# Seven products in the order 1, 6, 5, 2, 3, 7, 4, sums that always read one part from PSUM, one score step at a place, and the last head prepared in one piece

## The chip, the cores and the metric

The kernel runs on one core of a Trainium2 chip. Its engines are TensorE (PE, with its weight loads shown as PEld), VectorE (DVE), ScalarE (ACT), GpSimd (POOL) and SyncE (SP), which issues nearly all DMAs. Each engine works through its own queue in order. The metric is the device time of one execution in microseconds (us).

## The reference

A masked attention is followed by a mixture of experts. Batch 2, 8 heads, 768 rows, head dimension 64; the second part sees 1536 rows of 512, 4 experts, inner width 1024.

```python
q_bits = (np.einsum('bhsd,dk->bhsk', q, proj) > 0)        # the same for k
mask = q_bucket[:, :, :, None] == k_bucket[:, :, None, :]  # bucket: the 6 bits as a number
scores = np.where(mask, scale * np.matmul(q, k.transpose(0, 1, 3, 2)), -1000000000.0)
attn = np.exp(scores - np.max(scores, axis=-1, keepdims=True))
attn = attn / (np.sum(attn, axis=-1, keepdims=True) + 1e-09)
x = np.matmul(attn, v)                                     # heads side by side: 1536 x 512
p = domain_probs / (domain_probs.sum(-1, keepdims=True) + 1e-09)
for e in range(4):
    h = np.maximum(x @ w1[e], 0.0)
    out += p[:, e:e + 1] * (h @ w2[e])
```

## The kernel before

**Stages.** The 16 heads (8 of each batch) pass through attention in steps of 128 rows, six a head: a score step on PE (`stage_s`, L441 and L443, into the PSUM tile `sps`), its clamp and row bound on DVE (L448), the exponential on ACT (L464), a turn of the result on DVE (L528) or PE, DMAs through DRAM, and the product with v on PE (L563, 24 matmuls into `pv`), whose result ACT (L590) and DVE (L588) copy out and POOL scales (L601). The mixture runs as 16 units, eight a batch; a unit is half of an expert's inner width. Its first layer multiplies x by a part of w1, its second layer (`product_2`, L783 to L785, six tiles of 12 matmuls into `mps`) multiplies the hidden values by a part of w2, and DVE adds each tile to `acc` (L777). All matmuls take their operands split into a high and a low part: three matmuls for a product.

**The order.** A program that is written out by hand sets it: `attention()` and `moe(b)` are generators. Each `yield` gives a cost, and after each place of the mixture the loop at the end of the kernel lets attention go on until its summed cost has caught up (`da` against `dm`). So attention of batch 1 runs among units 0 to 4 of batch 0, and what is left is drained in unit 5 (`drained`).

**The last head.** `prep_head` makes the operands of the next head: the scaled copy `ah` on ACT (L370), copies `q` (twice) and `k` of it on POOL (L258), the low part `al` on DVE (L373), `ah`'s first half from `al` on POOL (L258), the signs on ACT (L395, which empty the PSUM tile `hps` of the hash matmuls L385), and two small operations on POOL (L400, L258). For heads up to 14 this goes step by step beside the score steps. The last head (15) shares its tiles with head 14 (`ALONE`), so it is prepared between the last score step of one and the first of the other, with `yield`s in between and a gap of 2100 behind it.

**The fast units.** Units 4 to 15 (`unit_fast`) make the first layer with seven products instead of eight, twice a unit (j = 0 and 1, one half of the unit's width each). A product is 6 matmuls of 384 columns (L1064, L1067, L1068). Numbered by their operands: 1 is a11 b11, 2 a12 b21, 3 s4 b22, 4 a22 t4, 5 s1 t1, 6 s2 t2, 7 s3 t3. Before, their order is 1, 5, 6, 2, 3, 7, 4. Products 1 and 2 collect in the PSUM tile `pa`, 5 and 3 in `pd` (in the first batch all of them are called `mps`), 6, 7 and 4 have a tile each. ACT copies product 1 to SBUF (L1097) and product 5 (L1103); DVE makes the sums (L1107, L1114, L1119, L1120, L1127) in the SBUF tiles `mt`. Product 2 is added onto product 1 and product 3 onto product 5 in PSUM, so each must wait until the value before it has been copied out. A finished sum becomes hidden values: the high part `hh` by a Relu on ACT (`hidden_hi`, L1074), the low part `hl` on DVE (`hidden_lo`, L1079). The last sum of half j = 0 (after product 4) is made hidden in half j = 1, right behind its product 1. Beside that, `split_w2_fast` splits two pieces of w2 in each half, on ACT (L1049) and POOL (L1050). PSUM tiles of the kind `one` go round four buffers.

Of the kernel before, what the change touches and what calls it, by code (L numbers as in the profile page):

```python
# [8 lines left out]
F32 = mybir.dt.float32  # L9
F32R = mybir.dt.float32r  # L10
ACTF = mybir.ActivationFunctionType
ALU = mybir.AluOpType
# [35 lines left out]
SPLIT_FIRST = 3  # L48
FAST = 4
ALONE = 14  # L50
ALONE_GAP = 2100
EARLY = 5


# [1 line left out]
def tile_lsh_attention__then__domain_moe(  # L56
# [273 lines left out]
    def prep_head(b, h):  # L330
# [2 lines left out]

        def copies():
            for rows in (slice(0, D), slice(D, P)):
                copy_pool(q1[rows], ah[0:D].bitcast(F32))
            copy_pool(k2[0:D], ah[D:P].bitcast(F32))

        if second:
# [252 lines left out]
    def stage_m(b, h, g):  # L592
# [16 lines left out]
        if (h, g) == (H - 1, NT // G - 1):  # L609
            done_b[b] = True  # L610

    hseq = [(b, h) for b in range(B) for h in range(H)]
    seq = [(b, h, t) for b, h in hseq for t in range(NT)]
    done_b = [False] * B
# [11 lines left out]
    def attention():  # L626
        n = len(seq)
        prep = [iter(())]

        def do(op, i):  # L630
            if op == "N":
                j = i - LAG_N
                if 0 <= j < n:
                    stage_n(*seq[j])
            elif op == "R":
                for b in range(B):
                    for odd in range(2):
                        j = i - LAG_R[b][odd]
                        if 0 <= j < n and (seq[j][0], seq[j][1] % 2) == (b, odd):
                            stage_r(*seq[j])  # L640
            elif op == "T":
                j = i - LAG_T
                if 0 <= j < n and heavy(*seq[j]):
                    stage_t(*seq[j])
                    return 654
            elif op == "X":
                j = i - LAG_X
                if 0 <= j < n and not heavy(*seq[j]):
                    stage_x(*seq[j])
            elif op == "Y":  # L650
                j = i - LAG_Y
                if 0 <= j < n and j % G == G - 1 and not heavy(*seq[j]):
                    b, h, t = seq[j]
                    stage_y(b, h, t // G)
            elif op == "S":
                if i < n:
                    b, h, t = seq[i]
                    if t == 0:
                        x = hseq.index((b, h))
                        prep[0] = prep_head(*hseq[x + 1]) if x + 1 < len(hseq) else iter(())  # L660
                    stage_s(b, h, t)
                    return 652 + 4270 // NT
                return DRAIN
            elif op == "V":
                for bh, lag in ended(i):
                    for part, at in enumerate(v_lags(*bh)):
                        if lag == at:
                            stage_v(*bh, part, len(v_lags(*bh)))
                            if (bh, part) == ((0, H - 1), len(v_lags(*bh)) - 1):
                                ready[0] = True  # L670
                                return 0
            elif op == "U":
                for bh, lag in ended(i):
                    if lag == u_lag(*bh):
                        stage_u(*bh)
            elif op == "M":
                for (b, h), lag in ended(i):
                    for g in range(NT // G):
                        if h % 2 and lag == (u_lag(b, h) if (b, h) == (0, H - 1) else LAG_M[b] + g):
                            stage_m(b, h, g)  # L680
                if done_b[0] and ready[0]:
                    ready[0] = False
                    return 0
            elif op == "E":
                j = i - LAG_E
                if 0 <= j < n:
                    stage_e(*seq[j])
            elif op == "P":
                if i < n:
                    b, h, t = seq[i]  # L690
                    x = hseq.index((b, h))
                    c = next(prep[0], None) if t >= PREP_AT and x < ALONE else None
                    if t == NT - 1 and x + 2 < len(hseq) and in_blocks(*hseq[x + 2]) and x < ALONE:
                        turn_blocks(*hseq[x + 2])
                    if t == QK_AT and x + 2 < len(hseq):
                        load_qk(*hseq[x + 2])
                    if t == 1 and x:
                        load_v(*hseq[x])
                    return c
            return None  # L700

        for i in range(n + LAG_M[1] + 3):
            for op in ORDER:
                c = do(op, i)
                if c is not None:
                    yield c
            x, t = divmod(i, NT)
            if t == NT - 1 and ALONE <= x < len(hseq) - 1:
                for c in prep[0]:
                    yield c  # L710
                if x + 2 < len(hseq):
                    turn_blocks(*hseq[x + 2])
                yield ALONE_GAP

    wts = {}
    queue = [(g, i, c) for g in range(B * NU) for i in range(2) for c in range(0, KD, WC)]
# [339 lines left out]
    def unit_fast(b, u, first_u):  # L1056
# [33 lines left out]
        w = wts.pop((first_u + u, 0))  # L1090
        sp2 = split_w2_fast(first_u + u)
        ma, mb = (pair_tile([P, 2, SB], "mt") for _ in range(2))
        s1, u2, s5, u3 = ma[:, 0], ma[:, 1], mb[:, 0], mb[:, 1]
        for j in range(2):
            pa = acc("pa", 0)
            product(pa, w["a11"], xop["b11"], j, True)
            nc.scalar.activation(s1, pa, ACTF.Copy)  # L1097
            if j:
                hidden(0, 1 + j, u3)
            yield 1120  # L1100
            pd = acc("pd", 0)
            product(pd, w["s1"], xop["t1"], j, True)
            nc.scalar.activation(s5, pd, ACTF.Copy)  # L1103
            yield 1120
            pb = acc("mps", 1)
            product(pb, w["s2"], xop["t2"], j, True)
            nc.vector.tensor_tensor(out=u2, in0=pb, in1=s1, op=ALU.add)  # L1107
            yield 1120
            product(pa, w["a12"], xop["b21"], j, False)
            hidden(0, j, pa)  # L1110
            next(sp2, 0)
            yield 1120
            product(pd, w["s4"], xop["b22"], j, False)
            nc.vector.tensor_tensor(out=s1, in0=pd, in1=u2, op=ALU.add)  # L1114
            hidden_hi(1, j, s1)
            yield 1120
            pc = acc("mps", 1)
            product(pc, w["s3"], xop["t3"], j, True)
            nc.vector.tensor_tensor(out=u3, in0=pc, in1=u2, op=ALU.add)  # L1119
            nc.vector.tensor_tensor(out=s5, in0=u3, in1=s5, op=ALU.add)  # L1120
            hidden_hi(1, 2 + j, s5)
            hidden_lo(1, j, s1)
            hidden_lo(1, 2 + j, s5)
            yield 1120
            pe_ = acc("mps", 1)
            product(pe_, w["a22"], xop["t4"], j, True)
            nc.vector.tensor_tensor(out=u3, in0=u3, in1=pe_, op=ALU.subtract)  # L1127
            yield 1120
        hidden(0, 3, u3)
        for _ in sp2:  # L1130
            pass
# [8 lines left out]
    with tc.manual_schedule():  # L1140
# [28 lines left out]
        for b in range(B):  # L1169
            dm = da = 0.0  # L1170
            for c in moe(b):
                dm += c
                while da < dm * ATT_PACE * n_att / n_moe:
                    x = next(att, None)
                    if x is None:
                        break
                    da += x
            if b == 0:
                for _ in att:
                    pass  # L1180
# [28 lines left out]
```

## Time and profile before

| | us |
|---|---|
| median of 3 runs (719.26 to 720.13) | 719.74 |
| the profiled execution | 719.53 |
| its span in the profile | 717.6 |
| PE busy | 701.0 (98%) |
| DVE busy | 517.1 (72%) |
| ACT busy | 342.7 (48%) |
| POOL busy | 315.8 (44%) |

Busy time is summed over the span. PE's share is so high that only its idle stretches, and stretches at a lower granted clock, can be told from work that has to be done; where PE waits, the profile names the operation that released it. Attention alone fills the first 125 us or so. From there to about 378 us attention of batch 1 and the mixture of batch 0 share the engines, and from 466.5 us on the second batch's eight fast units follow each other.

### The profile page before, as it was taken

Reading aid. Unit: us, or ns where it says so; the run is one execution under the profiler, and the core shown is the slowest. Engines: PE = TensorE matmul, PEld = TensorE weight load, DVE = VectorE, ACT = ScalarE, POOL = GpSimd, SP = SyncE. Lnnn points to the kernel's source line nnn. Section 1 sums busy time; section 2 is a strip of 40 time slices with the busy share of each in tenths; the row PEclk is TensorE's granted clock in tenths of the full one; section 3 lists DMA queues with packets and bytes.
Section 4 is the critical chain, followed back from the end, with each engine's and each line's share of the span. In section 5 each row is a group of like instructions: output and inputs, shape, how many; then the busy total and the mean of one; then the engine's idle time right before and its main releaser. Section 6 shows DMA issues by size and latency. Waiting matters only on the chain.

```text
span 717.6 us, 10186 instructions
## 1 busy us (share of the span) xinstructions
PE 701.0 (98%) x3702; PEld 590.1 (82%) x3702; DVE 517.1 (72%) x816; ACT 342.7 (48%) x669; POOL 315.8 (44%) x290
## 2 busy tenths in 40 slices
PE   8999999999999999979899999999999999999998
PEld 6766765979888888848687889898998989899896
DVE  6898888856584677767766887866868576685863
ACT  6888787543543434524523344343534334343440
POOL 6359577523363344453324645523434233342420
PEclk9999999999999999979999999999999999999999
DMA  5423353769997797817862112242121221112202
GB/s 137 75 50 74 74 119 79 217 172 239 250 254 204 205 238 207 266 59 202 242 168 61 59 60 89 87 140 67 59 65 64 79 88 60 59 58 89 66 23 88
DMA packets 90849, 87.77 MB, mean 122 GB/s; under 512 B 53168, under 2 KB 55728, under 8 KB 90800
## 3 DMA queue, kind: packets, MB, share of 16 engines
q1 hardware_dynamic: 89776, 86.80, 43.7%
q8 instruction: 29, 0.48, 0.3%
q10 hardware_dynamic: 1024, 0.33, 0.2%
q14 instruction: 20, 0.16, 0.1%
HBM read 65.04 MB, written 22.07 MB: 121 GB/s over the span
## 4 chain that ended last, share of the span: by engine, by line
PE 84%; DVE 5%; POOL 5%; issue 3%; ACT 2%; DMA 1%; POOLq 0%; DVEq 0%; ACTq 0%
PE mps L783 11%; PE mps L785 11%; PE mps L784 11%; PE pv L563 8%; PE mps L1064 4%; PE mps L1068 4%; PE mps L1067 4%; PE sps L443 4%; PE ptps L509 4%; PE sps L441 3%; PE mps L831 3%; PE mps L833 3%; PE mps L832 3%; PE pa L1064 2%; PE pd L1064 2%
## 5 line engine op out<-in xcount | busy, mean ns | idle before, releaser
L785 PE MATMUL mps<-w2hi,hl 128*128 128x512 f32 (+1 forms) x388 | 151.5, 390 | 1.8 <-DVE hl L1079 1.8
L783 PE MATMUL mps<-w2hi,hh 128*128 128x512 f32 (+1 forms) x388 | 152.2, 392 | 0.1
L784 PE MATMUL mps<-w2lo,hh 128*128 128x512 f32 (+1 forms) x388 | 151.4, 390 | 0.0
L1050 POOL TENSOR_TENSOR w2lo<-ws,w2hi 128x512 fp32r<-128x512 f32 x48 | 61.3, 1300 | 152.0 <-ACT w2hi L1049 141.3
L448 DVE TENSOR_SCALAR_CACHE_REDUCE p<-sps 128x768 f32<-128x768 f32 x96 | 90.1, 939 | 19.7 <-PE sps L443 18.0
L777 DVE SCALAR_TENSOR_TENSOR acc<-mps,pe,acc 128x512 f32<-128x512 f32 (+1 forms) x85 | 62.8, 739 | 50.8 <-PE mps L785 50.6
L464 ACT ACTIVATE p<-p,nb 128x768 f32<-128x768 f32 x96 | 89.4, 932 | 19.8 <-DVE p L448 19.4
L785 PEld LDWEIGHTS mps<-w2hi,hl 128*128 128x128 f32 x388 | 73.4, 189 | 18.7 <-DVE hl L1079 2.2
L783 PEld LDWEIGHTS mps<-w2hi,hh 128*128 128x128 f32 x388 | 73.4, 189 | 16.3 <-issue 1.2
L784 PEld LDWEIGHTS mps<-w2lo,hh 128*128 128x128 f32 x388 | 73.5, 189 | 14.1
L1008 POOL TENSOR_TENSOR w1lo<-ws,w1hi 128x512 fp32r<-128x512 f32 x36 | 52.1, 1453 | 53.4 <-issue 41.4
L1074 ACT ACTIVATE hh<-mt 128x384 fp32r<-128x384 f32 x72 | 37.8, 525 | 72.7 <-DVE mt L1120 43.8
L563 PE MATMUL pv<-pt,tv 128*64 128x384 f32 x288 | 67.2, 492 | 0.0
L1004 ACT ACTIVATE w1hi<-wc 128x512 fp32r<-128x512 f32 x48 | 30.1, 631 | 66.5 <-DVE wc L1013 66.4
L441 PE MATMUL sps<-ah,q 128*128 128x384 f32 x192 | 54.1, 363 | 2.6 <-POOL ah L258 2.3
L1079 DVE SCALAR_TENSOR_TENSOR hl<-mt,hh 128x384 fp32r<-128x384 f32 x72 | 42.8, 596 | 16.3 <-ACT hh L1074 13.6
L443 PE MATMUL sps<-k,al 76*128 76x384 f32 x192 | 50.3, 342 | 3.7 <-POOL k L258 3.3
L563 PEld LDWEIGHTS pv<-pt,tv 128*64 128x64 f32 x288 | 24.9, 137 | 32.5 <-issue 31.1
L258 POOL TENSOR_SCALAR q<-ah 64x768 fp32r<-64x768 f32 (+1 forms) x33 | 28.1, 853 | 52.6 <-ACT ah L370 38.4
L528 DVE STREAM_TRANSPOSE t<-p 128x768 f32<-128x768 f32 x48 | 46.2, 963 | 5.9 <-ACT p L464 5.9
L1068 PE MATMUL mps<-xo,w1lo 128*128 128x384 f32 x144 | 48.5, 337 | 0.0
L1067 PE MATMUL mps<-xo,w1hi 128*128 128x384 f32 x144 | 48.4, 336 | 0.0
(158 smaller groups left out, 1555.6 us busy)
## 6 DMA issues: line engine op xcount, KB each, us to landing
ws<-in_moe_w_dram SPq DMA_DIRECT2D x64, 512.0 KB, 3.9
scr<-t SPq DMA_DIRECT2D x16, 1152.0 KB, 8.4
pt<-scr SPq DMA_DIRECT2D x64, 288.0 KB, 6.0
tv<-in_v_dram SPq DMA_DIRECT2D x16, 192.0 KB, 3.0
tqk<-in_q_dram SPq DMA_DIRECT2D x30, 96.0 KB, 3.1
out_dram<-acc SPq DMA_DIRECT2D x11, 256.0 KB, 2.0
tqk<-in_k_dram SPq DMA_DIRECT2D x28, 96.0 KB, 3.3
rdb<-row SPq DMA_DIRECT2D x14, 192.0 KB, 5.6
```

Of the source, the lines that this page charges most:

```text
L441: nc.tensor.matmul(ps[:, i, :NH], q1[:, sl], k1[:, i * NH : (i + 1) * NH], start=True, stop=False)
L443: nc.tensor.matmul(ps[:, i, :NH], q2[0:MQE, sl], k2[0:MQE, i * NH : (i + 1) * NH], start=False, stop=True)
L448: nc.vector.tensor_scalar(out=two(pt), in0=ps[:, :, :NH], scalar1=MASKED, scalar2=MASKED, op0=ALU.min, op1=ALU.min, accum_out=nb,)
L464: nc.scalar.activation(pt, pt, ACTF.Exp, bias=nb, scale=-1.0, accum_out=dens[b, h, r][:, o : o + 1])
L563: nc.tensor.matmul(dst, vvs[b, h][:, c], pts[b, h, g][c], start=c == 0, stop=c == NT - 1, tile_position=(0, g * D),)
L777: nc.vector.scalar_tensor_tensor(out=acc, in0=ps, scalar=pcol, in1=acc, op0=ALU.mult, op1=ALU.add)
L783: nc.tensor.matmul(ps, hh[:, ts], w2hi[:, f, cs], start=n == 0, stop=False)
L784: nc.tensor.matmul(ps, hh[:, ts], w2lo[:, f, cs], start=False, stop=False)
L785: nc.tensor.matmul(ps, hl[:, ts], w2hi[:, f, cs], start=False, stop=n == FC - 1)
L1050: nc.gpsimd.tensor_tensor(out=lo[:, c + o], in0=t[:, o], in1=hi[:, c + o].bitcast(F32), op=ALU.subtract)
L1067: nc.tensor.matmul(ps, whi[:, kk, fs], xl[kk], start=False, stop=False, skip_group_check=True)
L1068: nc.tensor.matmul(ps, wlo[:, kk, fs], xh[kk], start=False, stop=kk == KH - 1, skip_group_check=True)
```

## The change

Five things change.

- In a fast unit product 6 comes before product 5. Product 5 is no longer copied to SBUF by ACT: DVE adds it to the sum of 1 and 6 straight from PSUM (`c22`), and the sum of two SBUF tiles (L1120) becomes a second sum that reads product 7 from PSUM. ACT has one copy less in each half, DVE one sum more.
- The low part `hl` of a hidden value follows its high part at once (`hidden` in place of `hidden_hi` now and `hidden_lo` later).
- A half of a unit has two places for attention (`SLOT` 3920 each) instead of seven (1120 each), and attention makes one score step at a place at most (`S_COST`).
- The last head is prepared in one piece at one place; the costs of its steps are summed onto the gap, which goes from 2100 to 3400.
- The last head's two `q` copies go from POOL to ACT.

```diff
-ALONE_GAP = 2100
+SLOT = 3920
+ALONE_GAP = 3400
@@ prep_head, copies
-                copy_pool(q1[rows], ah[0:D].bitcast(F32))
+                if b * H + h > ALONE:
+                    nc.scalar.activation(q1[rows], ah[0:D].bitcast(F32), ACTF.Copy)
+                else:
+                    copy_pool(q1[rows], ah[0:D].bitcast(F32))
@@ attention
-                for c in prep[0]:
-                    yield c
+                gap = sum(prep[0], ALONE_GAP)
                 if x + 2 < len(hseq):
                     turn_blocks(*hseq[x + 2])
-                yield ALONE_GAP
+                yield gap
@@ unit_fast
-        s1, u2, s5, u3 = ma[:, 0], ma[:, 1], mb[:, 0], mb[:, 1]
+        u2, u3, c12, c22 = ma[:, 0], ma[:, 1], mb[:, 0], mb[:, 1]
         for j in range(2):
             pa = acc("pa", 0)
             product(pa, w["a11"], xop["b11"], j, True)
-            nc.scalar.activation(s1, pa, ACTF.Copy)
+            nc.scalar.activation(u2, pa, ACTF.Copy)
             if j:
                 hidden(0, 1 + j, u3)
-            yield 1120
-            pd = acc("pd", 0)
-            product(pd, w["s1"], xop["t1"], j, True)
-            nc.scalar.activation(s5, pd, ACTF.Copy)
-            yield 1120
+            yield SLOT
             pb = acc("mps", 1)
             product(pb, w["s2"], xop["t2"], j, True)
-            nc.vector.tensor_tensor(out=u2, in0=pb, in1=s1, op=ALU.add)
-            yield 1120
+            nc.vector.tensor_tensor(out=u2, in0=pb, in1=u2, op=ALU.add)
+            pd = acc("pd", 0)
+            product(pd, w["s1"], xop["t1"], j, True)
+            nc.vector.tensor_tensor(out=c22, in0=pd, in1=u2, op=ALU.add)
             product(pa, w["a12"], xop["b21"], j, False)
             hidden(0, j, pa)
             next(sp2, 0)
-            yield 1120
             product(pd, w["s4"], xop["b22"], j, False)
-            nc.vector.tensor_tensor(out=s1, in0=pd, in1=u2, op=ALU.add)
-            hidden_hi(1, j, s1)
-            yield 1120
+            nc.vector.tensor_tensor(out=c12, in0=pd, in1=u2, op=ALU.add)
+            hidden(1, j, c12)
+            yield SLOT
             pc = acc("mps", 1)
             product(pc, w["s3"], xop["t3"], j, True)
             nc.vector.tensor_tensor(out=u3, in0=pc, in1=u2, op=ALU.add)
-            nc.vector.tensor_tensor(out=s5, in0=u3, in1=s5, op=ALU.add)
-            hidden_hi(1, 2 + j, s5)
-            hidden_lo(1, j, s1)
-            hidden_lo(1, 2 + j, s5)
-            yield 1120
+            nc.vector.tensor_tensor(out=c22, in0=pc, in1=c22, op=ALU.add)
+            hidden(1, 2 + j, c22)
             pe_ = acc("mps", 1)
             product(pe_, w["a22"], xop["t4"], j, True)
             nc.vector.tensor_tensor(out=u3, in0=u3, in1=pe_, op=ALU.subtract)
-            yield 1120
@@ the loop at the end
                     da += x
+                    if x == S_COST:
+                        break
```

The instructions move only from the last head's preparation on. Three places follow.

On PE one more second-layer tile, four instead of three, now stands between the last head's hash matmuls and its first score step. On POOL, at that preparation (`q`, `k`, `ah` and `al` are the head's operands, `w1lo` and `w2lo` low parts of weights), the queue before is:

```order
L258 TENSOR_SCALAR q_3338<-ah 64x768 x2
L258 TENSOR_SCALAR k_3341<-ah 64x768
L258 TENSOR_SCALAR ah<-al 64x768
L1008 TENSOR_TENSOR w1lo_3295<-ws,w1hi_3294 128x512
L400 TENSOR_SCALAR al<-k_3341,bit_mul 44x768
L258 TENSOR_SCALAR k_3341<-al 12x768
L1008 TENSOR_TENSOR w1lo_3295<-wc,w1hi_3294 128x512
```

and now:

```order
L259 TENSOR_SCALAR k_3341<-ah 64x768
L259 TENSOR_SCALAR ah<-al 64x768
L404 TENSOR_SCALAR al<-k_3341,bit_mul 44x768
L259 TENSOR_SCALAR k_3341<-al 12x768
L1012 TENSOR_TENSOR w1lo_3295<-ws,w1hi_3294 128x512
```

The two `q` copies are gone to ACT, where they stand between the scaled copy and the signs, and the weight's low part no longer comes between the head's own four operations.

On DVE in unit 4, the one fast unit that shares the engines with score steps (`p<-sps` is the clamp of a score step, `t<-p` a turn, `mt` the sums, `hl` low parts), the queue before is, from the low part of `pa` in half 0 to the first sum of half 1:

```order
L1079 SCALAR_TENSOR_TENSOR hl<-mps,hh 128x384
L1114 TENSOR_TENSOR mt<-mps,mt 128x384
L1119 TENSOR_TENSOR mt<-mps,mt 128x384
L1120 TENSOR_TENSOR mt<-mt 128x384
L1079 SCALAR_TENSOR_TENSOR hl<-mt,hh 128x384 x2
L528 STREAM_TRANSPOSE t_3480<-p 128x6x4x32
L448 TENSOR_SCALAR p,nb<-sps 128x768
L1127 TENSOR_TENSOR mt<-mt,mps 128x384
L1079 SCALAR_TENSOR_TENSOR hl<-mt,hh 128x384
L528 STREAM_TRANSPOSE t_3599<-p 128x6x4x32
L448 TENSOR_SCALAR p,nb<-sps 128x768
L1107 TENSOR_TENSOR mt<-mps,mt 128x384
```

and now, from the sum behind product 7 in half 0 to the sum of product 5 in half 1 (five rows stand ahead of these since product 3: a sum, its low part, the copy of `pv`, a turn and a clamp):

```order
L1120 TENSOR_TENSOR mt<-mps,mt 128x384
L1121 TENSOR_TENSOR mt<-mps,mt 128x384
L1083 SCALAR_TENSOR_TENSOR hl<-mt,hh 128x384
L1125 TENSOR_TENSOR mt<-mt,mps 128x384
L1083 SCALAR_TENSOR_TENSOR hl<-mt,hh 128x384
L479 TENSOR_SCALAR den<-den 128x6
L480 RECIPROCAL rd<-den 128x6
L532 STREAM_TRANSPOSE t_3525<-p 128x6x4x32
L452 TENSOR_SCALAR p,nb<-sps 128x768
L1107 TENSOR_TENSOR mt<-mps,mt 128x384
L1110 TENSOR_TENSOR mt<-mps,mt 128x384
```

The sum that reads product 5 (L1110) is new on DVE and stands behind all of these; before, ACT made the copy that product 3 waits for.

On DVE in a fast unit of the second batch, the queue before is, from the sum behind product 3 of half 0 to the first sum of half 1:

```order
L1114 TENSOR_TENSOR mt<-pd,mt 128x384
L1119 TENSOR_TENSOR mt<-mps,mt 128x384
L1120 TENSOR_TENSOR mt<-mt 128x384
L1079 SCALAR_TENSOR_TENSOR hl<-mt,hh 128x384 x2
L1127 TENSOR_TENSOR mt<-mt,mps 128x384
L1079 SCALAR_TENSOR_TENSOR hl<-mt,hh 128x384
L1107 TENSOR_TENSOR mt<-mps,mt 128x384
```

and now, to the sum of product 5 of half 1:

```order
L1115 TENSOR_TENSOR mt<-pd,mt 128x384
L1083 SCALAR_TENSOR_TENSOR hl<-mt,hh 128x384
L1120 TENSOR_TENSOR mt<-mps,mt 128x384
L1121 TENSOR_TENSOR mt<-mps,mt 128x384
L1083 SCALAR_TENSOR_TENSOR hl<-mt,hh 128x384
L1125 TENSOR_TENSOR mt<-mt,mps 128x384
L1083 SCALAR_TENSOR_TENSOR hl<-mt,hh 128x384
L1107 TENSOR_TENSOR mt<-mps,mt 128x384
L1110 TENSOR_TENSOR mt<-pd,mt 128x384
```

The low part of the first sum has moved ahead of the sum behind product 7, and the row at the end, L1110, is what product 3 of half 1 waits for.

## Rows read from the trace of the kernel before

**Rows 1.** Waits of PE: releaser, us in total, times, longest us.

```profile
PE mps L1064 <- ACT mt L1103: 2.4, 1, 2.4
...
PE mps L785 <- DVE hl L1079: 1.8, 1, 1.8
```

**Rows 2.** Timeline of PE, 307.7 to 321: start, duration, instruction, idle before.

```profile
307.74 0.39 PE L783 MATMUL mps<-w2hi,hh 128*128 128x512 f32 x1
...
308.19 0.39 PE L785 MATMUL mps<-w2hi,hl 128*128 128x512 f32 x1
310.84 1.01 PE L441 MATMUL sps<-ah,q 128*128 128x384 f32 x2 [2.27 <-POOL ah L258]
314.79 1.01 PE L443 MATMUL sps<-k,al 76*128 76x384 f32 x2 [2.94 <-POOL k L258]
315.59 0.63 PE L783 MATMUL mps<-w2hi,hh 128*128 128x512 f32 x1
...
320.85 4.14 PE L563 MATMUL pv<-pt,tv 128*64 128x384 f32 x24
```

**Rows 3.** Windows: length, busy us of PE, PEld, DVE, ACT, POOL, granted clock, DMA.

```profile
310.00:312.00 2.00, 1.01 (x2) 0.50 (x2) 2.00 (x4) 1.24 (x3) 1.92 (x2) 0.69 0.19 57
...
340.00:342.00 2.00, 0.32 (x2) 0.00 (x0) 1.41 (x4) 1.11 (x2) 0.00 (x0) 1.00 1.05 221
...
497.40:528.30 30.90, 30.90 (x157) 28.04 (x157) 21.93 (x31) 12.28 (x23) 11.09 (x8) 1.00 0.22 69
```

**Rows 4.** Timeline of ACT, DVE and POOL at the last head's preparation.

```profile
304.59 0.92 ACT L370 ACTIVATE ah<-xt,qk_scale 128x768 fp32r<-128x768 f32 x1
...
305.54 1.18 ACT L395 ACTIVATE k<-hps,sgn_bias 44x384 fp32r<-44x384 f32 x2
305.60 2.70 POOL L258 TENSOR_SCALAR q<-ah 64x768 fp32r<-64x768 f32 x2 [3.05 <-ACT ah L370]
306.03 1.58 DVE L373 SCALAR_TENSOR_TENSOR al<-xt,qk_scale,ah 128x768 fp32r<-128x768 f32 x1
...
309.53 1.26 POOL L258 TENSOR_SCALAR ah<-al 64x768 fp32r<-64x768 f32 x1
...
312.60 1.22 POOL L400 TENSOR_SCALAR al<-k,bit_mul 44x768 fp32r<-44x768 f32 x1
...
313.90 0.83 POOL L258 TENSOR_SCALAR k<-al 12x768 fp32r<-12x768 f32 x1
```

**Rows 5.** Groups of DVE: count, busy us, mean ns of one, idle before.

```profile
L448 DVE TENSOR_SCALAR_CACHE_REDUCE p<-sps 128x768 f32<-128x768 f32 x96 | 90.1, 939 | 19.7 <-PE sps L443 18.0
...
L528 DVE STREAM_TRANSPOSE t<-p 128x768 f32<-128x768 f32 x48 | 46.2, 963 | 5.9 <-ACT p L464 5.9
...
L1120 DVE TENSOR_TENSOR mt<-mt 128x384 f32<-128x384 f32 x24 | 32.3, 1348 | 0.8
```

**Rows 6.** Timelines of DVE, POOL and ACT in the fast unit that starts at 497.46.

```profile
502.86 0.56 DVE L1114 TENSOR_TENSOR mt<-pd,mt 128x384 f32<-128x384 f32 x1
...
504.49 1.45 DVE L1120 TENSOR_TENSOR mt<-mt 128x384 f32<-128x384 f32 x1
...
502.96 2.56 POOL L1050 TENSOR_TENSOR w2lo<-ws,w2hi 128x512 fp32r<-128x512 f32 x2 [8.22 <-ACT w2hi L1049]
...
515.99 2.99 POOL L1008 TENSOR_TENSOR w1lo<-ws,w1hi 128x512 fp32r<-128x512 f32 x2 [3.24 <-issue]
...
516.50 1.33 DVE L1013 TENSOR_TENSOR wc<-ws 128x512 f32<-128x512 f32 x1
...
503.45 0.53 ACT L1074 ACTIVATE hh<-mt 128x384 fp32r<-128x384 f32 x1
...
508.02 0.47 ACT L1103 ACTIVATE mt<-pd 128x384 f32<-128x384 f32 x1
```

**Rows 7.** Timeline of PE in the same unit: products 2 and 3 of half 1 start.

```profile
507.86 0.34 PE L1064 MATMUL pa<-xo,w1hi 128*128 128x384 f32 x1
...
508.90 0.34 PE L1064 MATMUL pd<-xo,w1hi 128*128 128x384 f32 x1
```

More of the change, by code (lines that the diff above doesn't have):

```diff
@@ L610, in stage_m @@
             done_b[b] = True
+    S_COST = 652 + 4270 // NT
     hseq = [(b, h) for b in range(B) for h in range(H)]
@@ L661, in do @@
                     stage_s(b, h, t)
-                    return 652 + 4270 // NT
+                    return S_COST
                 return DRAIN
@@ L1096, in unit_fast @@
             product(pa, w["a11"], xop["b11"], j, True)
-            nc.scalar.activation(s1, pa, ACTF.Copy)
+            nc.scalar.activation(u2, pa, ACTF.Copy)
             if j:
                 hidden(0, 1 + j, u3)
-            yield 1120
+            yield SLOT
+            pb = acc("mps", 1)
+            product(pb, w["s2"], xop["t2"], j, True)
+            nc.vector.tensor_tensor(out=u2, in0=pb, in1=u2, op=ALU.add)
             pd = acc("pd", 0)
             product(pd, w["s1"], xop["t1"], j, True)
-            nc.scalar.activation(s5, pd, ACTF.Copy)
-            yield 1120
-            pb = acc("mps", 1)
-            product(pb, w["s2"], xop["t2"], j, True)
-            nc.vector.tensor_tensor(out=u2, in0=pb, in1=s1, op=ALU.add)
-            yield 1120
+            nc.vector.tensor_tensor(out=c22, in0=pd, in1=u2, op=ALU.add)
             product(pa, w["a12"], xop["b21"], j, False)
```

## The prediction

> **What bounds the kernel now.** I read the waits of PE first. PE is busy for 98% of the span, so only its few idle stretches can be won, and any new one is paid in full. Two of the larger waits stand in [rows 1]: 2.43 us in unit 4, where product 3 waits for ACT's copy of product 5, and 1.78 in unit 5, where a second-layer matmul waits for a low part `hl`. The other two are in the timeline of PE at the last head's preparation [rows 2]: 2.27 before the first half of the score step, and 2.94 before the second. I read the windows next [rows 3]. Behind those waits the granted clock is 0.69 of full and then 0.5, that is, the lower of its two levels, and a second-layer matmul takes 0.63 where it took 0.39. In unit 4, with 1.68 of 2 us idle, the clock stays at 1.00. The last window is a whole fast unit of the second batch, with PE busy 30.90 of 30.90 us. There are ten such units (6 and 7 of the first batch, eight of the second), and none has anything to win. What the change does to them can only be nothing or a loss. Last I read the timelines of the other engines, since every term below is a race of one of them against PE.
>
> **The last head.** From the end of the tile before (its last start 308.19, plus 0.39) to the product with v (320.85) PE spends 12.27 us. The work in it is one tile, 12 matmuls at 0.227 each (three starts apart 0.45 for two), 2.72, and the score step, four matmuls of 384 columns at 0.173 (a sixth of the pitch of a product, 1.04, [rows 7]), 0.70. So 8.85 is lost: 5.21 idle, 3.64 by the clock.
>
> Now the change [rows 4]. The two `q` copies leave POOL (2.70), and no weight part stands between POOL's four operations. On ACT the `q` copies cost about 0.92 each, as the scaled copy L370 of twice the partitions and equal length does. ACT ends `ah` at 305.51, the copies at 307.35, the signs (1.18) at 308.5. On POOL the first `k` copy and `ah` from `al` are over by 308.9 (`al` ends at 307.6, plus 1.26), the bit product (1.22) by 310.1, the last copy (0.83) by 310.95. PE has one more tile to do meanwhile: 308.42 + 2.72 = 311.14. The cover is thin, 0.2 us, and the fourth tile may wait some 0.1 to 0.3 for the PSUM tile that the signs empty at 308.5. I take **−8.5**, between −8.85 and −5.2 (a short wait that still brings the lower clock, 3.64). If the cover is gone, every tenth of POOL's chain is a tenth of PE's.
>
> **Unit 4.** Here DVE also serves score steps. Before, product 3 of half 1 waits 2.43 for ACT. After, it waits for DVE's new sum L1110, which queues behind everything from product 3 of half 0 on: eight sums and low parts, the copy of `pv`, itself, ten rows at 0.56 [rows 6], 5.6; two turns at 0.96 and two clamps at 0.94 [rows 5], 3.8; and two Relus of ACT at 0.53 that low parts wait for, with hand-offs 1.35 by estimate. That is 10.75. PE has in that time six products at 1.04 and two score steps at 0.70, 7.65, so it waits 3.1. Behind it I add three smaller waits of one DVE row each (a PSUM tile that a late row empties, the next tile, the first second-layer tile), 1.6. So 4.7 in place of 2.4, **+2.3**. The ends: −2.4, if DVE's rows overlap more than I think, and +5.
>
> **Unit 5.** The low part of the first sum now comes at once, ahead of the sums behind product 7. I take 0.5 in place of 1.78, **−1.3** (−1.8 to 0).
>
> **The ten full units.** This is the term that decides. Take the traced unit's times [rows 6]. Half 0's sum c12 runs on DVE from 502.86 to 503.42. ACT's Relu of it ends at 503.98 (it stands behind the two `w2hi` copies, as before). DVE's next row is now its low part, which reads two SBUF tiles while POOL is busy from 502.96 with the first of two subtractions of 1.28 each, until 504.24. The trace shows what such a row does beside POOL: L1120 begins at 504.49 and takes 1.45, to 505.94, that is 0.42 past POOL's end at 505.52. So the low part ends near 504.24 + 0.42 = 504.66. Then follow on DVE, each behind the one before: the sum behind product 7, 505.22; the new `c22`, 505.78; its Relu on ACT, 506.31; its low part, 506.87; the sum behind product 4, 507.43; its Relu, 507.96; its low part, 508.52; product 6's sum of half 1, 509.08; and L1110, 509.64, or some 0.1 less by overlap of neighbouring rows. PE could start product 3 of half 1 at 508.90 [rows 7], as it does now (ACT's copy ended at 508.49, 0.41 before). So PE waits 0.65 to 0.75, once a unit. Half 0 has no such wait: DVE has been idle before it. At the second layer's start a low part of half 1, held up by POOL in the same way, is late by about 0.2. Together 0.9 a unit, **+9.0** for ten. The ends are 0 and 2.1 a unit (0.9 and the 1.28 of POOL's second subtraction, rounded), 0 to +21.
>
> The Trainium skill, "SBUF — State Buffer", section "SBUF: two separate sides", says that VectorE and GpSimd share one pair of ports by an exclusive lock: a VectorE row with two SBUF inputs and a GpSimd row that reads SBUF do not overlap, and the one that starts later waits for the whole of the other. The trace agrees in L1120's mean of 1.35 over 24 [rows 5]. The rule speaks against this change, since it moves a row of that kind into POOL's stretch; if POOL's second subtraction, too, counts as started first, the rule gives rival C's time in place of the sum's.
>
> **The clock.** Three us of idle in unit 4 may bring the lower clock. 2.43 idle did not [rows 1, 3], 2.27 and 2.94 close together did, and cost 3.64. I take **+0.8**, 0 to +3.6.
>
> **Removed and added for nothing.** ACT's 24 copies of 0.47 go and no one waited for them but in unit 4; PE's instructions are the same in number; the places for attention change what runs ahead of what only from the last head on.
>
> **Sum.** −8.5 + 2.3 − 1.3 + 9.0 + 0.8 = +2.3. On the profiled execution (719.53; span 717.6 and 1.9 around it) that is 721.8, and with the median 0.21 above that execution, **722.0**.
>
> **Rivals.**
> - *A, the other side: no wait in the full units.* DVE reaches L1110 by 508.90, with 6.04 us behind c12's start where I count 6.7. It decides at that one point: if the rows that follow each other overlap by 0.1 each, 0.7 goes. Then 722.0 − 9.0 = 713.0. Against it: three Relus stand inside the chain, and their hand-offs are only partly in my count.
> - *B: the low part is not held by POOL.* Then 0.45 a unit, 722.0 − 4.5 = 717.5. Against it is L1120's 1.45; for it, that L1120 is a sum, and these rows show no low part that starts beside a POOL row.
> - *C: POOL's second subtraction goes first as well,* and the low part ends 1.28 later; about 1.1 a unit more, 733.0. Against it: at 515.99 two POOL rows take 2.99 where two take 2.56 otherwise, with a DVE row of 1.33 started at 516.50 [rows 6], so DVE gets in between two of POOL's.
> - *D: the lower clock lasts in unit 4,* +3.6 in place of 0.8: 724.8.
> - That the change does not do what it says is excluded for the order, which the queues show. That the last head gains less is in its bounds.
>
> **How the numbers follow.** The forecast has 0.50, with a range of its own from 718.5 to 726 (0.6 to 1.2 a unit, and unit 4 by its bounds); A 0.17, B 0.15, C 0.06, D 0.12. From 714.0 to 727.5 the range takes in B, D, the forecast and the upper part of A (0.1 of a wait left a unit), and leaves out C and most of A, 0.19. A measurement of this kernel can tell about 0.2% from no change, 718.3 to 721.2. Faster is A, two thirds of B and a little of the forecast, 0.29; the same is the rest of B and the forecast's lower part, 0.20; slower 0.51.
>
> **What would show it.** In the profile after: PE's wait for L1110 at product 3, some ten times 0.65 and one of about 3 in unit 4; no wait of note at the last score step and the clock at 1.00 near 310; unit 5's wait for `hl` at a third; the second sum behind product 7 at 0.56, and the low part of c12 ending 0.4 past a POOL subtraction. I am wrong on the whole if full units show no wait of PE, or if the last head's chain still ends behind the tile.

## The result, and the profile after

The changed kernel takes 723.57 us (median of 4 runs, 723.31 to 723.66) against 719.62 (719.26 to 720.13) for the kernel before on the same chip: a ratio of 1.0054, interval 1.0036 to 1.0071. It is slower by 3.9 us; the forecast was 722.0, slower by 2.3. The profiled execution took 723.31, its span is 721.6 against 717.6. On the chip of the repeat below the executions of the kernel before run from 719.3 us, at a mean granted clock of 0.994, to 722.9, at 0.990, so ratios from two chips can be compared to some 2 us and no closer.

PE's busy time, 705.1 us, is again 98% of the span, so the sum shows nothing. The waits do. From the view of PE's waits after the change (releaser, us in total, times, longest us; L1068 is a matmul of a product, L1110 the new sum):

```profile
PE mps L1068 <- DVE mt L1110: 4.4, 3, 3.7
PE pd L1068 <- DVE mt L1110: 4.0, 8, 0.5
...
PE sps L447 <- POOL k L259: 0.4, 1, 0.4
```

None of the waits of [rows 1] is left. In their place PE waits for the new sum L1110: once in each of the eight units of the second batch, 0.50 as the profile counts it, and three times in the first batch, in units 4, 6 and 7. The last head's waits are down to 0.4.

**The full units.** The same unit as in [rows 3], in the windows view (length, busy us of PE, PEld, DVE, ACT, POOL, granted clock, DMA):

```profile
495.27:527.07 31.80, 31.30 (x157) 27.92 (x156) 21.80 (x33) 11.17 (x21) 11.37 (x8) 1.00 0.21 67
```

A unit is 31.80 long where it was 30.92, with the granted clock at 1.00. DVE is not busier than before (21.80 against 21.93): two sums of two SBUF tiles, 1.45 and 1.39, are gone and four sums of 0.56 have come, and still the unit is longer. The timelines of DVE, POOL and PE between the first sum of half 0 and product 3 of half 1 (start, duration, instruction, idle before):

```profile
500.67 0.56 DVE L1115 TENSOR_TENSOR mt<-pd,mt 128x384 f32<-128x384 f32 x1
501.82 0.67 DVE L1083 SCALAR_TENSOR_TENSOR hl<-mt,hh 128x384 fp32r<-128x384 f32 x1 [0.59 <-ACT hh L1078]
502.41 0.55 DVE L1120 TENSOR_TENSOR mt<-mps,mt 128x384 f32<-128x384 f32 x1
502.88 0.54 DVE L1121 TENSOR_TENSOR mt<-mps,mt 128x384 f32<-128x384 f32 x1
504.01 0.56 DVE L1083 SCALAR_TENSOR_TENSOR hl<-mt,hh 128x384 fp32r<-128x384 f32 x1 [0.59 <-ACT hh L1078]
504.49 0.55 DVE L1125 TENSOR_TENSOR mt<-mt,mps 128x384 f32<-128x384 f32 x1
505.62 0.56 DVE L1083 SCALAR_TENSOR_TENSOR hl<-mt,hh 128x384 fp32r<-128x384 f32 x1 [0.59 <-ACT hh L1078]
506.10 0.55 DVE L1107 TENSOR_TENSOR mt<-mps,mt 128x384 f32<-128x384 f32 x1
506.76 0.56 DVE L1110 TENSOR_TENSOR mt<-pd,mt 128x384 f32<-128x384 f32 x1
...
500.77 2.87 POOL L1054 TENSOR_TENSOR w2lo<-ws,w2hi 128x512 fp32r<-128x512 f32 x2 [8.12 <-ACT w2hi L1053]
...
506.53 0.34 PE L1072 MATMUL pa<-xo,w1lo 128*128 128x384 f32 x1
507.37 0.44 PE L1068 MATMUL pd<-xo,w1hi 128*128 128x384 f32 x1 [0.50 <-DVE mt L1110]
```

From the start of the first sum (500.67) to the end of L1110 (507.32) are 6.65 us. DVE stands still three times in it, 0.59 each, for a Relu of ACT. Between the start of the last matmul of product 2 and that of the first of product 3 are 0.84, where two starts are normally 0.17 apart (the pitch), so the true wait is 0.67; "0.50" is what is left after the modelled end of the matmul before. The matmul that restarts costs 0.11 more, and the first second-layer tile another 0.08: 0.86 of the unit's growth of 0.88.

**The last head.** On PE the fourth tile ends and the score step starts at 312.32; its second half and the next work follow (timeline of PE):

```profile
312.32 0.51 PE L445 MATMUL sps<-ah,q 128*128 128x384 f32 x2
312.86 0.61 PE L447 MATMUL sps<-k,al 76*128 76x384 f32 x2
313.31 0.34 PE L1068 MATMUL mps<-xs,w1hi 128*128 128x384 f32 x1
```

The step takes 0.99 instead of the 0.70 of its matmuls alone, and the window from 300 to 320 has the clock at 1.00 where [rows 3] had 0.69. Of the 8.85 us lost before [rows 2], 0.29 are left.

**Unit 4.** The timelines of DVE and PE ahead of product 3 of half 1, and the windows of PE behind it (length, busy us, granted clock):

```profile
331.49 0.56 DVE L1083 SCALAR_TENSOR_TENSOR hl<-mt,hh 128x384 fp32r<-128x384 f32 x1 [0.59 <-ACT hh L1078]
331.96 0.17 DVE L479 TENSOR_SCALAR den<-den 128x6 f32<-128x6 f32 x1
332.16 0.19 DVE L480 RECIPROCAL rd<-den 128x6 f32<-128x6 f32 x1
332.40 0.98 DVE L532 STREAM_TRANSPOSE t<-p 128x768 f32<-128x768 f32 x1
333.31 0.92 DVE L452 TENSOR_SCALAR_CACHE_REDUCE p<-sps 128x768 f32<-128x768 f32 x1
...
334.16 0.55 DVE L1107 TENSOR_TENSOR mt<-mps,mt 128x384 f32<-128x384 f32 x1
334.81 0.56 DVE L1110 TENSOR_TENSOR mt<-mps,mt 128x384 f32<-128x384 f32 x1
...
335.43 0.69 PE L1068 MATMUL mps<-xs,w1hi 128*128 128x384 f32 x1 [3.72 <-DVE mt L1110]
```

```profile
335.40:337.00 1.60, 1.57 (x5) 0.50 0.22 22
337.00:338.60 1.60, 1.60 (x7) 0.54 0.84 252
338.60:340.00 1.40, 1.40 (x10) 1.00 0.82 195
```

A turn and a clamp of a score step stand right ahead of the two sums, and PE waits 3.9 us (4.06 between the starts less 0.17), then works at the lower clock (0.50 and 0.54 granted) for 3.2 us.

**Where the 4.0 us of span came from.** The starts of the fast units in the two traces give the stages:

| stage | change, us | forecast |
|---|---|---|
| up to 190 us: a product with v waits for a transfer | +1.1 | – |
| last head, up to its first score step | −8.6 | −8.5 |
| from there to unit 5 (366.58 before, 362.77 after) | +3.7 | +2.3 and +0.8 |
| unit 5 | −1.7 | −1.3 |
| units 6 and 7 | +2.5 | +1.8 |
| the eight units of the second batch | +7.0 | +7.2 |

The first line stands at a place where the change moves nothing; whether it belongs to the change is asked below.

### The profile page after: what moved, and what is told of

It reads as the page before. It is cut to its first block, busy times and chain, and to the rows that moved or that the text cites. A ratio compares the mean times of both kernels' runs of the same rounds, so it can differ in the third digit from the quotient of the medians.

```text
span 721.6 us, 10160 instructions
## 1 busy us (share of the span) xinstructions
PE 705.1 (98%) x3702; PEld 588.1 (82%) x3702; DVE 515.4 (71%) x840; ACT 331.8 (46%) x647; POOL 317.9 (44%) x288
## 4 chain that ended last, share of the span: by engine, by line
PE 74%; DVE 14%; ACT 6%; DMA 2%; issue 2%; POOL 1%; SPq 0%; DVEq 0%; POOLq 0%; ACTq 0%
PE mps L787 11%; PE mps L789 10%; PE mps L788 10%; PE pv L567 9%; PE ptps L513 4%; PE sps L447 4%; PE sps L445 4%; DVE hl L1083 4%; ACT hh L1078 4%; PE mps L835 3%; PE mps L1068 3%; PE mps L837 3%; PE mps L836 3%; PE mps L1072 2%; PE mps L1071 2%
## 5 line engine op out<-in xcount | busy, mean ns | idle before, releaser
L1054 POOL TENSOR_TENSOR w2lo<-ws,w2hi 128x512 fp32r<-128x512 f32 x48 | 65.5, 1387 | 141.1 <-ACT w2hi L1053 139.8
L1083 DVE SCALAR_TENSOR_TENSOR hl<-mt,hh 128x384 fp32r<-128x384 f32 x72 | 46.9, 652 | 42.6 <-ACT hh L1078 42.6
L1068 PE MATMUL mps<-xo,w1hi 128*128 128x384 f32 x144 | 48.5, 337 | 0.0
L1071 PE MATMUL mps<-xo,w1hi 128*128 128x384 f32 x144 | 48.4, 336 | 0.0
```

What stands on the lines that cost most here:

```text
L1054: nc.gpsimd.tensor_tensor(out=lo[:, c + o], in0=t[:, o], in1=hi[:, c + o].bitcast(F32), op=ALU.subtract)
L1068: nc.tensor.matmul(ps, whi[:, kk, fs], xh[kk], start=first and kk == 0, stop=False, skip_group_check=True)
L1083: nc.vector.scalar_tensor_tensor(out=hl, in0=src, scalar=0.0, in1=hh.bitcast(F32), op0=ALU.max, op1=ALU.subtract)
```

## The experiments

The kernel before took 719.6 us on the first chip and 721.1 to 721.8 on those of the experiments, so each is given beside the kernel before of its own chip.

**The two parts apart.** First the last head's part alone on the kernel before (diff against the kernel before; the `q` copies on ACT as in the change):

```diff
+ALONE_GAP = 3400
-                for c in prep[0]:
-                    yield c
+                gap = sum(prep[0], ALONE_GAP)
...
-                yield ALONE_GAP
+                yield gap
```

> The kernel before with only the last head's part of the change: prepared in one piece, gap 3400, its two q copies on ACT; the fast units and their places as before. If the last head's 8.85 us are won as a part of their own, and the loss of the whole change sits in the fast units: 719.6 - 8.5 = 711, with a spread of 3 since a sixth score step now falls into unit 4. Rival: what is won there comes back later, because the score steps that PE no longer waits for only crowd unit 4: 717 to 720.

Measured 710.95 us beside 721.37, ratio 0.9862 (0.9843 to 0.9881). Then the rest alone, the change with this part undone:

> The changed kernel with the last head prepared as before (step by step, gap 2100, q copies on POOL). If the two parts add up: 723.6 + 8.5 = 732, full units 0.9 us longer each than before, PE's 2.3 and 2.9 us waits at the last head back. Rival: the parts overlap (the waits of unit 4 shrink when its score steps come later): 728 or less.

Measured 731.96 beside 721.37, ratio 1.0155 (1.0133 to 1.0177). Gain and loss are separate: −10.4 and +10.6 us on that chip. They add up to +0.2, under the whole (+3.9 on the first chip, +1.8 in the repeat below) by no more than chips differ. In the last head's part alone all of PE's remaining waits are small (view of PE's waits):

```profile
PE sps L444 <- DVE p L451: 1.8, 2, 1.5
```

The larger of the two, 1.5, is a score step in unit 4 that waits for the clamp of one before. In the other kernel, with the units alone, the waits for L1108 (there the number of L1110) and the old waits at the last head stand side by side:

```profile
PE mps L1066 <- DVE mt L1108: 7.0, 4, 3.7
PE pd L1066 <- DVE mt L1108: 4.4, 8, 0.9
PE sps L444 <- POOL k L259: 3.7, 2, 3.3
PE sps L442 <- POOL ah L259: 2.3, 1, 2.3
```

**The chain to L1110.** In half 1, the low part of half 0's last sum goes behind L1110 (diff against the changed kernel):

```diff
             if j:
-                hidden(0, 1 + j, u3)
+                hidden_hi(0, 1 + j, u3)
...
             nc.vector.tensor_tensor(out=c22, in0=pd, in1=u2, op=ALU.add)
+            if j:
+                hidden_lo(0, 1 + j, u3)
             product(pa, w["a12"], xop["b21"], j, False)
```

> The changed kernel, but in half 1 the low part of the last sum of half 0 is made behind the new sum L1110, not ahead of it (its Relu stays where it is). Theory, that the chain of ten DVE rows from the first sum to L1110 sets product 3 of half 1 in each full unit: the low part (0.56) and the Relu it waits for (0.53 and a hand-off) leave the chain, L1110 ends some 1.0 us sooner, ahead of PE, so its wait of 0.67 and the restart go: 723.6 - 10 x 0.78 = 715.8, and about 1 less in unit 4: 715. Rival 1, that the DVE is simply full in half 1, so that the row moved delays the rows behind it as much: within 2 of 723.6. Rival 2, that the low part held up by POOL is what is late: no change in the chain's start, so 720 or more.

Measured 714.50 beside 721.37, ratio 0.9912 (0.989 to 0.9935). A full unit of the second batch is as long as before the change, PE full:

```profile
493.50:524.39 30.89, 30.89 (x157) 28.08 (x156) 20.79 (x33) 11.28 (x21) 11.34 (x8) 1.00 0.22 68
```

The chain of nine rows (the expectation counted ten) ended 0.67 late; with one row of 0.56 and the Relu that it waits for out of it, the whole loss of these eight units is gone. DVE has room for the new sums, it only must not have them in this order. In units 6 and 7, which had grown by 1.4 and 1.1, 0.5 and 0.3 are left: there product 2 of half 0 still waits for ACT's copy of product 1. In unit 4 nothing was won, against the expectation: PE's wait is still 3.7. The timelines of DVE and ACT there tell why (in this kernel the turn ahead of the two sums, and what ACT does before it):

```profile
331.27 0.98 DVE L532 STREAM_TRANSPOSE t<-p 128x768 f32<-128x768 f32 x1 [1.20 <-ACT p L468]
...
329.79 0.53 ACT L1078 ACTIVATE hh<-mt 128x384 fp32r<-128x384 f32 x1 [0.71 <-DVE mt L1127]
330.22 0.92 ACT L468 ACTIVATE p<-p,nb 128x768 f32<-128x768 f32 x1
```

The low part is gone from its front, and DVE stands idle for 1.20 in its stead: the turn waits for ACT's exponential, and this stands in ACT's queue behind the Relu of half 0's last sum, which the edit left in its place. The turn starts 1.05 behind the last matmul of product 2, as late as in the changed kernel (1.03).

**The new sum itself.** Product 5 is copied out by ACT again (diff against the changed kernel):

```diff
-            nc.vector.tensor_tensor(out=c22, in0=pd, in1=u2, op=ALU.add)
+            nc.scalar.activation(c22, pd, ACTF.Copy)
...
-            nc.vector.tensor_tensor(out=c22, in0=pc, in1=c22, op=ALU.add)
+            nc.vector.tensor_tensor(out=c22, in0=u3, in1=c22, op=ALU.add)
```

> The changed kernel, but product 5 is copied out by ACT again, and the second sum behind product 7 is again the sum of two SBUF tiles; order of products, low parts and places as changed. Theory: L1110 (0.56) and its place behind product 6's sum leave DVE, but the SBUF sum meets POOL's second subtraction and ends about 0.6 later, so PE's wait in a full unit is 0.1 to 0.3 in place of 0.67: 723.6 - 5 = 718.6. Rival, that the order 1, 6, 5 is what costs: no gain, 723 to 725. Rival, that the added sum is the whole cost: no wait left, 715.

Measured 717.34 beside 721.37, ratio 0.9948 (0.993 to 0.9966). A full unit is 31.19, 0.3 longer than before the change:

```profile
492.29:523.48 31.19, 31.19 (x157) 27.87 (x156) 21.18 (x31) 12.17 (x23) 11.57 (x8) 1.00 0.20 68
```

The order 1, 6, 5 is not what costs, as it is kept here, and putting the copy back on ACT wins back two thirds of the unit's 0.88. What is left is not at product 3, where the expectation had it: 0.06 is lost there, and 0.19 at the second layer's first tile. The SBUF sum met POOL's second subtraction, as expected:

```profile
500.01 1.07 DVE L1121 TENSOR_TENSOR mt<-mt 128x384 f32<-128x384 f32 x1
...
497.80 2.87 POOL L1054 TENSOR_TENSOR w2lo<-ws,w2hi 128x512 fp32r<-128x512 f32 x2 [8.13 <-ACT w2hi L1053]
```

It ends at 501.08, 0.41 past POOL's end at 500.67.

**POOL's stretch.** The split of w2 starts later in each half (diff against the changed kernel):

```diff
             hidden(0, j, pa)
-            next(sp2, 0)
...
             hidden(1, j, c12)
+            next(sp2, 0)
```

> The changed kernel with the first split of w2 in each half moved from behind the Relu and low part of product 2's sum to behind those of product 3's, so that POOL's two subtractions start some 1.2 us later; nothing else. The low part of c12 is then free of POOL (0.11 us won), and the low part of c22, which reads two SBUF tiles too, starts while POOL is in its second subtraction. If such a row waits for the whole of POOL's row, as in unit 6 of one profile, it ends some 0.85 later, and with it all rows to L1110: PE's wait in a full unit goes from 0.67 to about 1.4, and 723.5 + 10 x 0.75 = 731. If VectorE and GpSimd rows only share and both slow a little: within 1.5 of 723.5. If POOL's stretch plays no part: the same as the changed kernel or 1 less.

Measured 742.84 beside 721.10, ratio 1.0293 (1.0264 to 1.0322): in the direction expected, and more of it. The DVE row that now meets POOL's stretch, and POOL's:

```profile
517.39 1.51 DVE L1083 SCALAR_TENSOR_TENSOR hl<-mt,hh 128x384 fp32r<-128x384 f32 x1 [0.59 <-ACT hh L1078]
...
515.93 2.55 POOL L1054 TENSOR_TENSOR w2lo<-ws,w2hi 128x512 fp32r<-128x512 f32 x2 [8.82 <-ACT w2hi L1053]
```

And of PE's waits in this kernel:

```profile
PE pd L1068 <- DVE mt L1110: 10.7, 8, 1.3
...
PE pv L567 <- DMA pt<-scr: 3.0, 1, 3.0
PE mps L1068 <- ACT mt L1101: 1.8, 2, 1.6
```

The low part ends at 518.90, 0.42 past POOL's end, 0.95 late. PE's wait at product 3 is 1.33 in place of 0.50, 0.83 more where 0.75 was expected. The unit is 2.06 longer than before the change, and not 1.65, because the same row of half 1 is held as well, which I had not priced: the first second-layer tile waits for it. The two profiles differ by 21.6 us: 9.3 in the eight units of the second batch, and 12.3 in units 4 to 7, where other work shares the engines. Of these, 3.0 are a product with v that stood for a transfer and 1.6 a wait for ACT's copy; the rest I did not follow up, so this run bears out the expected mechanism in the eight units and not its total.

**Unit 4's score step.** The first of a half's two places for attention goes behind L1110 (diff against the changed kernel):

```diff
-            yield SLOT
             pb = acc("mps", 1)
...
             nc.vector.tensor_tensor(out=c22, in0=pd, in1=u2, op=ALU.add)
+            yield SLOT
             product(pa, w["a12"], xop["b21"], j, False)
```

> The changed kernel with the first of a half's two places for attention moved from behind product 1 to behind the new sum L1110, so that in unit 4 the turn and the clamp of a score step stand behind that sum on DVE, not ahead of it. Nothing else; the full units have no attention in them and do not change. Theory, that unit 4's wait of 3.9 comes from these two rows, which themselves wait for ACT's exponential: the wait falls to about 1.7 (the low part ahead of the sum is still there), the lower clock behind it (1.6) goes, so 723.5 - 3.9 = 719.6. Rival, that the score steps only trade places and PE then waits for a clamp instead: within 1.5 of 723.5.

Measured 721.95 beside 721.78, ratio 1.0009 (0.9998 to 1.0021), and the changed kernel on the same chip:

> The changed kernel once more, on the chip of the next two, as their reference and for one question: in its first profile the product with v at 185.5 us stood still some 0.8 us for a transfer, at a place where the change moves nothing. If that was chance, this profile does not have it, and the span is about 1.1 shorter beside the kernel before (a ratio of 1.004); if it comes from the change, it is there again (1.0055).

723.53 beside 721.78, ratio 1.0026 (1.0014 to 1.0038). So the place is worth 1.6 us and not 3.9, close to what the rival had. PE's timeline in unit 4 with the later place:

```profile
328.65 0.44 PE L1068 MATMUL mps<-xs,w1hi 128*128 128x384 f32 x1 [0.83 <-DVE mt L1121]
...
332.55 0.44 PE L1068 MATMUL mps<-xs,w1hi 128*128 128x384 f32 x1 [0.81 <-DVE mt L1109]
...
340.33 0.51 PE L787 MATMUL mps<-w2hi,hh 128*128 128x512 f32 x1 [1.58 <-ACT hh L1078]
```

The 3.7 at product 3 have become 0.81 (L1109 is L1110 there), but two other waits grew. Product 5 waits 0.83 for L1121, which empties its PSUM tile (0.12 in the first trace): the score step that stood ahead of it on PE now comes after it. The second layer waits 1.58 for a Relu whose sum stands behind the turns and clamps on DVE. The lower clock did not come.

The repeat answers its question. Its product with v at the same place runs through in one piece (timeline of PE),

```profile
185.91 4.09 PE L567 MATMUL pv<-pt,tv 128*64 128x384 f32 x24
```

so the 1.1 us in the first line of the table was chance. From the start of unit 0 to that of unit 2, where all eleven runs have the same instructions, the first trace takes 98.3 us and eight of the others 97.2. The expectation's other half failed: the repeat's span is not 1.1 shorter but 0.9 longer (722.5), and the ratio is below both of its values. In unit 4 the lower clock lasted longer, up to 340.7 us, and cost 2.8 where it had cost 1.5. And unit 6 shows something that the first trace does not (timelines of DVE and POOL in the repeat):

```profile
406.13 1.70 DVE L1083 SCALAR_TENSOR_TENSOR hl<-mt,hh 128x384 fp32r<-128x384 f32 x1 [0.59 <-ACT hh L1078]
...
404.86 2.55 POOL L1054 TENSOR_TENSOR w2lo<-ws,w2hi 128x512 fp32r<-128x512 f32 x2 [1.01 <-ACT w2hi L1053]
```

and in the first trace:

```profile
405.67 0.56 DVE L1083 SCALAR_TENSOR_TENSOR hl<-mt,hh 128x384 fp32r<-128x384 f32 x1 [0.59 <-ACT hh L1078]
...
404.44 2.94 POOL L1054 TENSOR_TENSOR w2lo<-ws,w2hi 128x512 fp32r<-128x512 f32 x2 [1.04 <-ACT w2hi L1053]
```

In the repeat the low part of c12 began when POOL's first subtraction ended, and was held through the second, to 407.83, 0.42 past its end. In the first trace the same row was not held, and POOL's pair took longer. PE's wait behind it was 1.49 in the repeat and 0.34 in the first trace. The kernel with the last head's part undone and the one with the later place show the 1.49 in unit 6 as well.

**Both edits of the units together.**

> Both edits: the low part of half 0's last sum behind L1110, and the first place behind it too. Theory: no wait in the full units, and nothing of note at product 3 in unit 4: 714.5 - 3.9 - 1.6 = 709, a ratio of 0.983 to 0.985 to the kernel before, with the last head's gain kept; that would be below the last head's part alone (0.986). Rival, as for the run before: 713 to 715, a ratio near 0.991.

Measured 714.03 beside 721.78, ratio 0.9887 (0.9868 to 0.9906): between the two, nearer the rival. Its unit 4 has 1.98 of wait at the second layer, with the lower clock behind it, and 0.83 at product 5, in place of 3.7 at product 3. It does not reach the last head's part alone.

**What wins at the last head.** The last head's part alone, with the `q` copies left on POOL (diff against that kernel):

```diff
-                if b * H + h > ALONE:
-                    nc.scalar.activation(q1[rows], ah[0:D].bitcast(F32), ACTF.Copy)
-                else:
-                    copy_pool(q1[rows], ah[0:D].bitcast(F32))
+                copy_pool(q1[rows], ah[0:D].bitcast(F32))
```

> The last head's part alone (one piece, gap 3400, fast units as before), but with its two q copies left on POOL. Theory, that the one piece with its fourth tile covers the chain only because the copies left POOL: POOL's last copy ends 2.7 later, near 315, PE waits some 2.3 at the second half of the score step, with or without the lower clock behind it: 711 + 2.4 = 713.4 to 715.5 (a ratio of 0.989 to 0.992). Rival, that the one piece alone, with the weight's low part out of POOL's chain, is what wins: 711 again (0.986).

Measured 713.85 beside 721.10, ratio 0.99 (0.9876 to 0.9924), 2.7 us more than with the copies on ACT by the ratios. POOL's chain ends late and PE waits for it:

```profile
312.94 1.22 POOL L258 TENSOR_SCALAR k<-al 12x768 fp32r<-12x768 f32 x1
...
314.21 0.62 PE L443 MATMUL sps<-k,al 76*128 76x384 f32 x2 [1.84 <-POOL k L258]
```

So the larger part of the gain, 7.2 us, is the one piece with its tile more and a POOL queue without the weight's part (these two were not tried apart); moving the copies closes what is left.

## Why the prediction was right

**The last head, −8.5:** −8.6, but the size came by another way than the sum's. The two copies on ACT took 1.70 together and not 1.84, and `ah` from `al` 0.83 and not 1.26, but two operations of POOL took longer, its last copy among them (timeline of POOL):

```profile
311.63 1.18 POOL L259 TENSOR_SCALAR k<-al 12x768 fp32r<-12x768 f32 x1
```

The sum had 0.83 for this one, and 1.22 for the bit product ahead of it, which took 1.74. POOL ended at 312.81 and not 310.95, the tile at 312.32 and not 311.14 (1.1 of both the chance wait ahead). So the chain does end behind the tile, by 0.49, which the prediction gives as a sign that it is wrong on the whole: the cover of 0.2 was not there. It cost only 0.3, since the first half of the score step does not need POOL's last copy and runs meanwhile, and since the lower clock did not follow. The margin of 0.35 in −8.5 was taken with a wait of the fourth tile for the signs in mind, which did not come. Here the size was right in part by luck.

**The ten full units, +9.0:** +9.5. In the eight of the second batch the place, the releaser and the size were right: 0.67 of wait forecast as 0.65 to 0.75, and L1110's end 6.65 behind the start of the first sum where the sum had 6.7. Two small terms went against each other in it: the three hand-offs to a Relu took 0.59 where 0.53 stood in the sum, and rows that follow each other overlap by some 0.08. The 0.2 at the second layer was 0.08, and the restarting matmul's 0.11, which is not in the sum, made up for it. That moving one row takes the loss of these units away entirely shows the chain to be the cause. Units 6 and 7 grew by 1.4 and 1.1 and not by 0.9: L1110 costs 0.51 and a restart there, and product 2 of half 0 waits 0.3 to 0.4 for ACT's copy of product 1, which the forecast does not have. Rival A, without a wait in the full units, did not come, but the kernel with the low part behind L1110 met its condition in the second batch, and the price was about the one named: 9.0 forecast, 8 to 10 by the ratios (0.9912 against 1.0026 and 1.0054).

**Rival B was mispriced.** With the forecast's own numbers the low part that is not held ends at 503.98 + 0.56 = 504.54 and a hand-off, against 504.66 when it is held: 0.1 a unit, and not 0.45. The trace has 0.67 for it where 0.56 is free. It could never have brought the time to 717.5, and its 0.15 of chance belonged to the forecast.

**Rival C happened in unit 6.** There POOL's second subtraction went first in the repeat and in two kernels more, and PE's wait was 1.15 longer (1.49 against 0.34), forecast as 1.1; of the four traces with the changed kernel's chain to L1110 only the first was spared. The Trainium skill, "SBUF — State Buffer", section "SBUF: two separate sides", has it that of a VectorE row with two SBUF inputs and a GpSimd row that reads SBUF the one that starts first holds the shared ports for its whole instruction. The traces agree: every row held through a second subtraction here ends 0.41 to 0.42 past it. Who goes first when POOL has its next row waiting, they show too: in the eight units of the second batch DVE did, in both traces (0.67 or 0.68 in each), in unit 6 it was one or the other (the last section has the starts).

**Unit 4, +2.3 and +0.8 for the clock:** +3.7. The wait was 3.9 and not 3.1, since the chain has three gaps of 0.59 and one of 0.36 (for the exponential) where the sum took 1.35 for two; the three smaller waits came to 0.9 and not 1.6. The lower clock cost 1.5: six matmuls of product 3 and the score step of four at up to 0.32 pitch in place of 0.17, and the restart. The wait before, counted by the pitch too, was 2.6 and not 2.4. In the repeat the clock cost 2.8 and the smaller waits 0.4; both clock figures lie between the 0.8 taken and rival D's 3.6. The step that was incomplete is the list itself: it had the rows of DVE, and not ACT's Relu and exponential that the turn among them waits for, which is why taking a row out of the list moved nothing there.

**Unit 5, −1.3:** −1.7; the wait that was left at 0.5 did not come at all. **Chance, not in the sum:** +1.1 by a transfer in the profiled execution. Without it the forecast of +2.3 stands against +2.9 in that trace. Other chances went the other way in it: in the repeat unit 6 is 0.9 longer and unit 4 0.7. That the total lies so near the forecast is in part luck.

**A version that beats both** is the last head's part without the rest, 0.9862 of the kernel before. The sums from PSUM with the low part behind L1110 come to 0.9912: no loss in the eight units any more, but no gain either, as PE had none to give; most of the distance to 0.9862 is unit 4, 49.9 us long against 46.6.

## What to carry to other kernels

When PE has no idle time in a stage, work that is taken off DVE there is worth nothing (a unit was 30.9 long with DVE busy for 21.93 and for 20.79), and an added row is paid if it lands on the one chain that ends at PE's next release: follow that chain row by row, with every hand-off to another engine (0.59 of idle here for a Relu of 0.53), before counting busy time. A result that PE needs soon goes ahead of the one that is needed late; here the order of two rows on DVE was worth 8 to 10 us, a whole new sum less than that (5.6 to 7.6 by the ratios). And two edits of opposite sign in one change are told apart by the stage starts in two traces.

## What was not expected of the hardware

The lower clock does not follow the length of one idle stretch. The kernel before kept 1.00 through 2.43 us of idle in unit 4 [rows 1, 3], and the one with product 5's copy on ACT through 2.32; the kernel with both edits of the units lost it behind 1.98 (windows of PE there: length, busy us, granted clock, behind the wait that ended at 339.22):

```profile
339.20:341.00 1.80, 1.78 (x5) 0.58 0.98 220
341.00:343.00 2.00, 2.00 (x7) 0.52 1.05 224
```

And whether a DVE row gets in between two POOL rows or waits for both hung on a few hundredths of a us. In units 6 and 7 of six traces (all of the changed order but that with product 5's copy on ACT, and without the later split of w2) the low part of c12 starts 1.21 to 1.27 us behind POOL's first row of 1.28: seven rows that started at 1.21 to 1.25 were free, five at 1.25 to 1.27 ended 1.15 later.
